# The experts' first layers as seven block products in place of eight, in two passes over the weights

## The chip, the cores and the metric

The kernel runs on one core of one Trainium2 chip. The metric is the device time of one execution in microseconds (us); lower is better.

## The reference

```python
attn = memory_attention(q, k, v, phi)              # 4 x 8 heads x 576 tokens x 64
x = attn.transpose(0, 2, 1, 3).reshape(2304, 512)
h = np.maximum(x @ w_in, 0.0)                      # w_in 512 x 2048
x = h * h @ w_out                                  # w_out 2048 x 512
p = domain_probs / (domain_probs.sum(-1, keepdims=True) + 1e-09)
out = np.zeros((2304, 512))
for e in range(4):                                 # four experts
    h = np.maximum(x @ w1[e], 0.0)                 # w1 512 x 1024
    out += p[:, e:e + 1] * (h @ w2[e])             # w2 1024 x 512
```

Every expert runs on every token. The change is in the loop over the experts alone.

## The kernel before, in words

All products keep fp32 accuracy by a split: a value is held as a rounded high part and the remainder (xh and xl, gh and gl, the two halves of a tile of weights), and a product of two split operands is three matmuls: high x high, high x low, low x high.

The program has two stages. The first holds the attention and the first MLP; it ends with `first_l2` of the last slab, which leaves the tokens' activations in `acc` (seen as `yacc`) and splits them into xh and xl. The second stage is the experts. The hidden width of 4 x 1024 is cut into 16 slabs of 256 columns. For a slab `s`, five blocks of tokens are run, four of 512 and one of 256. For each block `second_l1` makes the slab's two 128-row halves of the hidden layer: 12 matmuls of 128 x 512 into one PSUM bank for each half (4 pieces of the 512 input rows, 3 matmuls for each), and then ScalarE's Relu (gh) and VectorE's remainder (gl). `second_l2` takes 128 tokens at a time: 6 matmuls into one bank, and VectorE adds the result, weighted by the expert's probability, to `acc` (on the first slab ScalarE writes it). The layer 2 of a block is queued in `pend` and is issued behind layer 1 of the next block, so that TensorE has 24 matmuls of layer 1 while the other engines finish a block.

Weights come by a generator, `weights()`: each `next(ws)` loads 256 KB of a slab, and `split` makes the high part (ScalarE, a cast) and the remainder (VectorE). A slab of the experts is four such tiles, loaded once for all 2304 tokens.

The Tile framework schedules: it sets the order of the instructions on each engine and the semaphores between them, and each engine works through its own list in order. PSUM has 8 banks: moe (3), fold (2), turn, memory and score; `CYCLE2` says which is next.

The functions that the change touches:

Of the kernel before, what the change touches and what calls it, by code (L numbers as in the profile page):

```python
# [32 lines left out]
HS = S // 2  # L33


@with_exitstack
def tile_kernel(
# [18 lines left out]
    CYCLE2 = itertools.cycle(("moe", "fold", "moe", "score", "moe", "fold", "memory", "turn"))  # L56
# [58 lines left out]
    def attention(att, g):  # L115
# [47 lines left out]
        for z in range(2):  # L163
# [23 lines left out]
        cols = slice(b * S, (b + 1) * S)  # L187
        nc.scalar.copy(xh[:, hg, cols], at)  # L188
        nc.vector.tensor_tensor(
            out=xh[:, 2 + hg, cols], in0=at, in1=xh[:, hg, cols].bitcast(F32), op=ALU.subtract  # L190
        )
# [36 lines left out]
    def split(w, name):  # L228
        t = wcp.tile([128, 2, WC], F32R, tag="wc", name=name)
# [38 lines left out]
    def fold(s, b):  # L268
        fs, o = SLABS1[s], b * S + offset(s)
# [3 lines left out]
        for h0 in range(0, 2, WC // fs):  # L273
            pf = bank("fold")
            groups = range(h0, h0 + WC // fs)
            for i, hg in enumerate(groups):
# [8 lines left out]
            hi = xl[:, h0:h0 + n, o:o + fs]  # L285
            nc.scalar.copy(hi, src)  # L286
            nc.vector.tensor_tensor(
                out=xl[:, 2 + h0:2 + h0 + n, o:o + fs], in0=src, in1=hi.bitcast(F32), op=ALU.subtract
            )

    def first_l1(s, j, pools, bk):
        hp, tmp = pools
        nf, b = SLABS1[s] // 128, j // 2
        o = b * S + offset(s)
        cs = slice(j * HS, (j + 1) * HS)
        gh = hp.tile([128, nf, HS], F32R, tag="gh", name="gh")
        gl = hp.tile([128, nf, HS], F32R, tag="gl", name="gl")
        for f in range(nf):
# [3 lines left out]
            for hg in range(2):  # L302
                for lw, rx in ((0, 0), (0, 2), (2, 0)):
                    nc.tensor.matmul(  # L304
                        ph[:, :HS], xl[:, lw + hg, fc], xh[:, rx + hg, cs], start=(i == 0), stop=(i == 5)
# [10 lines left out]
    def first_l2(s, j, g, bk):  # L316
# [3 lines left out]
        for d in range(KT):  # L320
# [14 lines left out]
            if s == N1 - 1:  # L335
                nc.scalar.copy(xh[:, d, cs], ya)
                nc.vector.tensor_tensor(
                    out=xl[:, d, cs], in0=ya, in1=xh[:, d, cs].bitcast(F32), op=ALU.subtract
                )


    def second_l1(s, c0, n, hp, bk):
        gh = hp.tile([128, NF2, NB], F32R, tag="gh", name="gh")
        gl = hp.tile([128, NF2, NB], F32R, tag="gl", name="gl")
        for f in range(NF2):
            ph = bk()
            i = 0
            w = w_two[s][f].rearrange("p h (k j) -> p h k j", k=KT)
            for k in range(KT):
                for lw, rx in ((0, xh), (0, xl), (1, xh)):  # L350
                    nc.tensor.matmul(  # L351
                        ph[:, :n], w[:, lw, k, :], rx[:, k, c0:c0 + n],
# [3 lines left out]
            nc.scalar.activation(gh[:, f, :n], ph[:, :n], AF.Relu)  # L356
            nc.vector.scalar_tensor_tensor(  # L357
                out=gl[:, f, :n], in0=ph[:, :n], scalar=0.0, in1=gh[:, f, :n].bitcast(F32),
                op0=ALU.max, op1=ALU.subtract,
            )  # L360
        return gh, gl

    def second_l2(s, c0, n, g, bk):
        gh, gl = g
        e = s // SE
        for q in range(n // 128):
            po = bk()
            i = 0
            ts = slice(q * 128, (q + 1) * 128)
            for f in range(NF2):  # L370
                w = w_two[s][NF2 + f]
# [156 lines left out]
```

## Time and profile before

| | |
|---|---|
| median of 3 runs | 1211.18 us (1210.82 to 1212.43) |
| the profiled execution | 1212.83 us, of which its span (first to last instruction) is 1211.0 us |
| TensorE matmul | busy 1185.9 us, 98% of the span, 6552 matmuls |
| VectorE | 651.7 us, 54% |
| ScalarE | 357.6 us, 30% |
| GpSimd | 1.9 us, 0% |

A matmul's row is longer than the time between two starts, because matmuls are pipelined: the next one starts before the modelled end of the one before. What a matmul costs is therefore read as the distance from one start to the next.

### The profile page before, as it was taken

The page shows a single profiled execution, that of the slowest core. Times are in us where ns is not written, and L with a number is a line of the kernel's source. Part 1 is how long each engine was busy: PE and PEld are TensorE (multiplying, and loading weights), DVE is VectorE, ACT ScalarE, POOL GpSimd, SP SyncE. Part 2 cuts the span into 40 slices and gives each one's busy share as a digit, 9 for nine tenths or more (in the row PEclk, how much of TensorE's full clock was granted, in tenths as well). Part 3 has the DMA queues.
Part 4 walks back from the last instruction along what each step waited for, and adds up shares of the span by engine and source line. Part 5 has one row for each costly group of instructions (what it writes and reads, how often), then busy time and mean ns, then how long its engine had stood idle before and what let it go on. Part 6 is the DMA issues. An engine that isn't in the chain of part 4 may idle for free.

```text
span 1211.0 us, 15894 instructions
## 1 busy us (share of the span) xinstructions
PE 1185.9 (98%) x6552; PEld 998.1 (82%) x6552; DVE 651.7 (54%) x1162; ACT 357.6 (30%) x827; POOL 1.9 (0%) x9
## 2 busy tenths in 40 slices
PE   4899999999999999999999999999999999999998
PEld 2677898898899988888888888888888888888887
DVE  5988999695455513444444444444444444444434
ACT  3676554454465442111111111111111111111110
POOL 0000000000000000000000000000000000000000
PEclk9899999999999999999999999999999999999999
DMA  8741222120010100001000010000100001000003
GB/s 303 257 147 53 70 71 87 54 79 10 1 36 1 35 9 26 18 18 36 18 18 18 18 35 18 18 29 7 35 18 18 35 1 35 18 18 18 1 35 122
DMA packets 25336, 55.84 MB, mean 46 GB/s; under 512 B 2992, under 2 KB 2992, under 8 KB 25264
## 3 DMA queue, kind: packets, MB, share of 16 engines
q1 hardware_dynamic: 25264, 54.84, 13.3%
q8 instruction: 51, 0.84, 0.3%
q14 instruction: 21, 0.17, 0.0%
HBM read 50.11 MB, written 4.72 MB: 45 GB/s over the span
## 4 chain that ended last, share of the span: by engine, by line
PE 96%; DVE 2%; DMA 1%; ACT 0%; issue 0%; SPq 0%
PE moe L373 13%; PE moe L351 11%; PE moe L326 9%; PE fold L373 9%; PE fold L351 6%; PE score L351 6%; PE turn L351 5%; PE memory L351 5%; PE moe L304 5%; PE memory L373 4%; PE turn L373 4%; PE score L373 4%; PE turn L326 3%; PE fold L278 3%; PE score L326 3%; PE memory L326 2%
## 5 line engine op out<-in xcount | busy, mean ns | idle before, releaser
L373 PE MATMUL moe<-w,gh 128*128 128x512 f32 x444 | 137.4, 390 | 0.0
L351 PE MATMUL moe<-xh,w 128*128 128x512 f32 (+1 forms) x456 | 135.2, 363 | 0.0
L326 PE MATMUL moe<-gh,wo 128*128 128x288 f32 x576 | 131.8, 299 | 1.7 <-ACT acc L332 1.2
L356 ACT ACTIVATE gh<-moe 128x512 fp32r<-128x512 f32 (+1 forms) x57 | 30.6, 537 | 344.8 <-PE moe L351 344.8
L357 DVE SCALAR_TENSOR_TENSOR gl<-moe,gh 128x512 fp32r<-128x512 f32 (+1 forms) x57 | 35.1, 617 | 130.0 <-ACT gh L356 130.0
L326 PEld LDWEIGHTS moe<-gh,wo 128*128 128x128 f32 x576 | 97.3, 188 | 8.2 <-ACT acc L332 3.8
L373 PEld LDWEIGHTS moe<-w,gh 128*128 128x128 f32 x444 | 82.8, 188 | 18.1
L373 PE MATMUL fold<-w,gh 128*128 128x512 f32 x316 | 97.3, 389 | 0.0
L351 PEld LDWEIGHTS moe<-xh,w 128*128 128x128 f32 x456 | 82.4, 188 | 14.8
L383 DVE SCALAR_TENSOR_TENSOR acc<-moe,p_sb,acc 128x512 f32<-128x512 f32 x104 | 78.1, 750 | 30.8 <-PE moe L373 28.0
L373 PE MATMUL moe<-w,gl 128*128 128x512 f32 x222 | 86.7, 391 | 0.0
L326 PE MATMUL moe<-gl,wo 128*128 128x288 f32 x288 | 85.1, 296 | 0.0
L351 PE MATMUL moe<-xl,w 128*128 128x512 f32 (+1 forms) x228 | 82.7, 363 | 0.0
L304 PE MATMUL moe<-xh,xl 128*128 128x288 f32 x432 | 75.0, 306 | 4.8 <-ACT xh L188 4.8
L313 DVE TENSOR_TENSOR gl<-g,gh 128x288 fp32r<-128x288 f32 x128 | 57.9, 454 | 36.7 <-ACT gh L312 35.6
L304 PEld LDWEIGHTS moe<-xh,xl 128*128 128x128 f32 x432 | 62.4, 192 | 17.9 <-ACT xl L286 7.6
L383 DVE SCALAR_TENSOR_TENSOR acc<-fold,p_sb,acc 128x512 f32<-128x512 f32 x74 | 55.5, 750 | 37.2 <-PE fold L373 37.2
L351 PE MATMUL fold<-xh,w 128*128 128x512 f32 (+1 forms) x264 | 71.1, 341 | 0.0
L373 PEld LDWEIGHTS fold<-w,gh 128*128 128x128 f32 x316 | 59.3, 188 | 12.3
L351 PE MATMUL score<-xh,w 128*128 128x512 f32 x192 | 64.2, 395 | 0.0
L351 PE MATMUL turn<-xh,w 128*128 128x512 f32 x184 | 61.6, 395 | 0.0
L351 PE MATMUL memory<-xh,w 128*128 128x512 f32 x184 | 61.5, 395 | 0.0
(141 smaller groups left out, 2244.4 us busy)
## 6 DMA issues: line engine op xcount, KB each, us to landing
raw<-in_wts SPq DMA_DIRECT2D x64, 256.0 KB, 2.5
raw<-in_wts SPq DMA_DIRECT2D x28, 512.0 KB, 3.3
kv<-in_kv SPq DMA_DIRECT2D x28, 256.0 KB, 4.0
acc<-in_qT SPq DMA_DIRECT2D x16, 288.0 KB, 5.2
out<-acc SPq DMA_DIRECT2D x18, 256.0 KB, 2.0
ph<-in_phiT SPq DMA_DIRECT2D x8, 288.0 KB, 4.4
acc<-in_wts SPq DMA_DIRECT2D x4, 512.0 KB, 6.3
acc<-in_kv SPq DMA_DIRECT2D x4, 256.0 KB, 7.0
```

What stands on the lines that cost most here:

```text
L278: nc.tensor.matmul(pf[pr * 64:(pr + 1) * 64, i * fs:(i + 1) * fs], bdv[:, 2 * b + hg, pr, :], k_of(2 * hg + pr), start=True, stop=True,)
L304: nc.tensor.matmul(ph[:, :HS], xl[:, lw + hg, fc], xh[:, rx + hg, cs], start=(i == 0), stop=(i == 5))
L313: nc.vector.tensor_tensor(out=gl[:, f], in0=g, in1=gh[:, f].bitcast(F32), op=ALU.subtract)
L326: nc.tensor.matmul(po[:, :HS], w[:, lw], rg[:, f], start=(i == 0), stop=(i == 3 * nf - 1))
L351: nc.tensor.matmul(ph[:, :n], w[:, lw, k, :], rx[:, k, c0:c0 + n], start=(i == 0), stop=(i == 3 * KT - 1),)
L356: nc.scalar.activation(gh[:, f, :n], ph[:, :n], AF.Relu)
L357: nc.vector.scalar_tensor_tensor(out=gl[:, f, :n], in0=ph[:, :n], scalar=0.0, in1=gh[:, f, :n].bitcast(F32), op0=ALU.max, op1=ALU.subtract,)
L373: nc.tensor.matmul(po, lg[:, f, ts], w[:, rw], start=(i == 0), stop=(i == 3 * NF2 - 1))
L383: nc.vector.scalar_tensor_tensor(out=oa, in0=po, scalar=pe, in1=oa, op0=ALU.mult, op1=ALU.add)
```

## The change

The tokens 0 to 2047 are run in two passes of 1024; a pass goes through all 16 slabs. In a pass the 1024 tokens are a pair of blocks of 512, the 512 input rows are two halves of 256, and the slab's hidden 256 columns are two halves of 128. Layer 1 of a slab on a pair is then a 2 x 2 by 2 x 2 block product. Instead of eight block products (48 matmuls of 512 columns) there are seven (42), by Strassen's algorithm in the form with few sums:

- of the weights, four sums of 128 x 256 are made for each slab in each pass, on GpSimd, in a tile `s4` that has one buffer; they are split as weights are (`ws`), so a slab has six split tiles in a pass, not four. Every slab is loaded twice, in loads of 512 KB (`ra` for layer 1, `rb` for layer 2);
- of the activations, `prepare` makes the seven operands of a pass (b11, b21, t1, t4, t2, t3, b22) once: 8 subtractions on VectorE, and 14 splits of 128 x 512 (ScalarE and VectorE). xh and xl are gone; the operands lie in slots of a tile `mem`, in the place that the attention's output and the folded weights held before;
- of the products, the seven go into four banks u, v, m and t. ScalarE copies u out three times while it goes on being added to, VectorE makes four sums of a bank and a copy (`total`: c11, c22, c21, c12), and Relu and remainder are then taken from the sum in SBUF (`rectified`). The product b22 is added into bank m after c22 was read from it;
- layer 2 is the same number of matmuls. Its eight tiles of a pair are put behind layer 1 of the next pair, in two halves, by `between`. It has four banks for itself;
- the last 256 tokens are run as before (`second_rest`), in the second pass, ahead of each pair.

```diff
-    CYCLE2 = itertools.cycle(("moe", "fold", "moe", "score", "moe", "fold", "memory", "turn"))
+    CYCLE2 = itertools.cycle(("fold", "turn", "fold", "memory"))
...
+        for ps_, s in itertools.product(range(2), range(S2)):
+            key = ps_, s
+            r = raw.tile([128, 2 * WC], F32, tag="raw", name=f"ra{ps_}_{s}")
+            nc.sync.dma_start(out=r, in_=wts[s, :, :2 * WC])
+            w_two[key] = [split(r[:, f * WC:(f + 1) * WC], f"w1{ps_}_{s}_{f}") for f in range(2)]
+            yield
+            a11, a12, a21, a22 = (r[:, i * 256:(i + 1) * 256] for i in range(4))
+            t = cp[0].tile([128, 4, 256], F32, tag="s4", name="s4", bufs=1)
+            nc.gpsimd.tensor_tensor(out=t[:, 0], in0=a21, in1=a22, op=ALU.add)
+            nc.gpsimd.tensor_tensor(out=t[:, 1], in0=t[:, 0], in1=a11, op=ALU.subtract)
+            nc.gpsimd.tensor_tensor(out=t[:, 2], in0=a11, in1=a21, op=ALU.subtract)
+            nc.gpsimd.tensor_tensor(out=t[:, 3], in0=a12, in1=t[:, 1], op=ALU.subtract)
+            for i in range(2):
+                u = t[:, 2 * i:2 * i + 2].rearrange("p i n -> p (i n)")
+                w_two[key].append(split(u, f"ws{ps_}_{s}_{i}"))
...
+    def put(dst, src):
+        nc.scalar.copy(dst[0], src)
+        nc.vector.tensor_tensor(out=dst[1], in0=src, in1=dst[0].bitcast(F32), op=ALU.subtract)
...
+        def product(po, name, first=True):
+            wb, xb = block(*a[name]), x[name]
+            i = 0
+            for k in range(2):
+                for lw, rx in ((0, 0), (0, 1), (1, 0)):
+                    nc.tensor.matmul(
+                        po, wb[lw][k], xb[:, rx, k], start=(first and i == 0), stop=(i == 5),
+                        skip_group_check=not first,
+                    )
+                    i += 1
+
+        def total(p, q):
+            c = cp[0].tile([128, NB], F32, tag="c", name="c")
+            nc.vector.tensor_tensor(out=c, in0=p, in1=q, op=ALU.add)
+            return rectified(c, NB)
...
+        u, v, m, t = bank("moe"), bank("moe"), bank("moe"), bank("score")
+        product(u, "b11")
+        u1 = copied(u)
+        product(v, "b21")
+        c11 = total(v, u1)
+        product(m, "t1")
+        product(t, "t4")
+        product(u, "t2", first=False)
+        u2 = copied(u)
+        between(0)
+        product(u, "t3", first=False)
+        u3 = copied(u)
+        c22 = total(m, u3)
+        c21 = total(t, u3)
+        between(1)
+        product(m, "b22", first=False)
+        c12 = total(m, u2)
...
+        for ps_ in range(2):
+            for s in range(S2):
+                if ps_:
+                    todo += second_rest(s, xr, between)
+                todo += second_pair(ps_, s, x, between)
+                for _ in range(3):
                     next(ws, None)
-        flush()
+            if ps_ == 0:
+                xr = rest()
+                for x in prepare(1):
+                    pass
+        between(1)
```

How the order of the instructions moves is shown at three places. In these rows L351 and L373 are the matmuls of layers 1 and 2 before, L471, L517 and L432 those of the pairs, of the last 256 tokens and of layer 2 in the changed kernel; "waits" names the engine waited for, and "xN" means N instructions.

The first place is TensorE in the second stage, before: the second half of a block's layer 1 in slab 6, and the first matmuls of layer 2 behind it.

```order
L351 MATMUL score_7028<-xh_72,w2_6_1_6822 128x512 [waits DVE_49]
L351 MATMUL score_7028<-xl_73,w2_6_1_6822 128x512
L351 MATMUL score_7028<-xh_72,w2_6_1_6822 128x512 x2
L351 MATMUL score_7028<-xl_73,w2_6_1_6822 128x512
L351 MATMUL score_7028<-xh_72,w2_6_1_6822 128x512 x2
L351 MATMUL score_7028<-xl_73,w2_6_1_6822 128x512
L351 MATMUL score_7028<-xh_72,w2_6_1_6822 128x512 x2
L351 MATMUL score_7028<-xl_73,w2_6_1_6822 128x512
L351 MATMUL score_7028<-xh_72,w2_6_1_6822 128x512
L373 MATMUL moe_7043<-w2_6_2_6891,gh_6963 128x512 [waits DVE_49,Activation_49]
```

In the changed kernel a pair of the first pass stands there, here slab 3, from its first product (u is moe_5460, v moe_5461, m moe_5462, t score_5463).

```order
L471 MATMUL moe_5460<-mem_72,w10_3_0_5435 128x512 x6
L471 MATMUL moe_5461<-mem_72,w10_3_0_5435 128x512 [waits Activation_49]
L471 MATMUL moe_5461<-mem_72,w10_3_0_5435 128x512 x5
L471 MATMUL moe_5462<-mem_72,ws0_3_0_5446 128x512 [waits DVE_49]
L471 MATMUL moe_5462<-mem_72,ws0_3_0_5446 128x512 x5
L471 MATMUL score_5463<-mem_72,w10_3_1_5438 128x512 x6
L471 MATMUL moe_5460<-mem_72,ws0_3_0_5446 128x512 [waits Activation_49]
L471 MATMUL moe_5460<-mem_72,ws0_3_0_5446 128x512 x5
L432 MATMUL fold_5503<-w20_2_0_5291,g_5317 128x512 x3
L432 MATMUL fold_5503<-w20_2_1_5294,g_5387 128x512 x3
```

Two groups of 12 became products of 6, with a wait at the head of most of them; four tiles of layer 2 of slab 2 follow (24 matmuls), then the product t3, four more tiles, the product b22, and the next pair.

The second place is VectorE in the second stage, before: additions to `acc` (L383), remainders (L357) and splits of weights (L231).

```order
L383 SCALAR_TENSOR_TENSOR acc_74<-moe_7319,p_sb_81,acc_74 128x512 [waits PE_49]
L231 TENSOR_TENSOR w2_8_2_7539<-raw2_8_2_7537,w2_8_2_7539 128x512 [waits DMAHW3_49,Activation_49]
L383 SCALAR_TENSOR_TENSOR acc_74<-fold_7327,p_sb_81,acc_74 128x512 [waits PE_49]
L231 TENSOR_TENSOR w2_8_3_7608<-raw2_8_3_7606,w2_8_3_7608 128x512 [waits DMAHW4_49,Activation_49]
L357 SCALAR_TENSOR_TENSOR gl_7336<-memory_7337,gh_7335 128x512 [waits Activation_49]
L357 SCALAR_TENSOR_TENSOR gl_7336<-turn_7352,gh_7335 128x512 [waits Activation_49]
```

In the changed kernel, from the sum c22 of pair 3 to its sum c12 (L479 the sums, L453 the remainders, L443 the additions to `acc`, L231 the splits of slab 4's layer 2 weights).

```order
L479 TENSOR_TENSOR c_5543<-moe_5462,cc_5541 128x512 [waits Activation_49]
L479 TENSOR_TENSOR c_5548<-score_5463,cc_5541 128x512
L443 SCALAR_TENSOR_TENSOR acc_73<-fold_5553,p_sb_74,acc_73 128x512 [waits PE_49]
L453 SCALAR_TENSOR_TENSOR g_5545<-c_5543,g_5545 128x512 [waits Activation_49]
L453 SCALAR_TENSOR_TENSOR g_5550<-c_5548,g_5550 128x512 [waits Activation_49]
L443 SCALAR_TENSOR_TENSOR acc_73<-turn_5561,p_sb_74,acc_73 128x512 [waits PE_49]
L443 SCALAR_TENSOR_TENSOR acc_73<-fold_5569,p_sb_74,acc_73 128x512 [waits PE_49]
L231 TENSOR_TENSOR w20_4_0_5617<-rb0_4_5615,w20_4_0_5617 128x512 [waits DMAHW2_49,Activation_49]
L443 SCALAR_TENSOR_TENSOR acc_73<-memory_5577,p_sb_74,acc_73 128x512 [waits PE_49]
L231 TENSOR_TENSOR w20_4_1_5620<-rb0_4_5615,w20_4_1_5620 128x512 [waits Activation_49]
L479 TENSOR_TENSOR c_5591<-moe_5462,cc_5501 128x512 [waits PE_49]
```

Behind c12 stand the second split of `ws` of slab 5, the remainder of c12, then c11 of pair 4 and its remainder, three splits of slab 6 (two of `ra`, the first of `ws`), and the four additions of the next half of layer 2: 22 instructions from one c22 to the next. Before, a slab had no sums and four splits.

The third place is TensorE in the second pass, where the last 256 tokens' layer 2 (fold_8200 and turn_8226) stands between the products, since the pair's own layer 2 has been issued ahead of it.

```order
L432 MATMUL fold_8200<-w21_2_0_8055,g_8106 128x512 [waits DVE_49]
L432 MATMUL fold_8200<-w21_2_0_8055,g_8106 128x512 x2
L432 MATMUL fold_8200<-w21_2_1_8058,g_8154 128x512 x3
L471 MATMUL moe_8157<-mem_72,ws1_2_1_8050 128x512 [waits Activation_49]
L471 MATMUL moe_8157<-mem_72,ws1_2_1_8050 128x512 x5
L432 MATMUL turn_8226<-w21_2_0_8055,g_8106 128x512 [waits DVE_49]
L432 MATMUL turn_8226<-w21_2_0_8055,g_8106 128x512 x2
L432 MATMUL turn_8226<-w21_2_1_8058,g_8154 128x512 x3
L517 MATMUL moe_8272<-mem_72,w11_3_0_8247 128x256 [waits DVE_49]
L471 MATMUL moe_8159<-mem_72,ws1_2_1_8050 128x512 [waits DVE_49]
L471 MATMUL moe_8159<-mem_72,ws1_2_1_8050 128x512 x5
L517 MATMUL moe_8272<-mem_72,w11_3_0_8247 128x256 x11
```

Here one tile of layer 2 stands between the product t2 and t3 (moe_8157, L471) and one tile and one short matmul between t3 and b22 (moe_8159), where the first pass has four tiles at each of the two places.

At the change from the first to the second pass VectorE has 13 instructions of `prepare` between the remainder of the last c12 and the first addition to `acc` of that pair's layer 2. In the last slab of the first MLP the 8 subtractions and 14 splits of the first pass's operands stand among that slab's work, where 32 splits of 128 x 288 stood before.

## Rows read from the trace of the kernel before

**Rows 1.** The page, parts 1 and 2: busy us of each engine; slices in tenths.

```profile
PE 1185.9 (98%) x6552; PEld 998.1 (82%) x6552; DVE 651.7 (54%) x1162; ACT 357.6 (30%) x827; POOL 1.9 (0%) x9
PE   4899999999999999999999999999999999999998
PEclk9899999999999999999999999999999999999999
```

**Rows 2.** The page, part 4: the chain that ended last, by engine.

```profile
PE 96%; DVE 2%; DMA 1%; ACT 0%; issue 0%; SPq 0%
```

**Rows 3.** Windows: the last slab of the first MLP, and 600 us of the experts.

```profile
core 0: us, PE busy (x) PEld busy (x) DVE busy (x) ACT busy (x) POOL busy (x), PEclk, DMA share, GB/s
371.40:409.70 38.30, 38.30 (x290) 38.30 (x289) 21.43 (x49) 20.73 (x56) 0.00 (x0) 1.00 0.01 1
500.00:1100.00 600.00, 600.00 (x2752) 495.90 (x2751) 270.23 (x387) 95.17 (x172) 0.00 (x0) 1.00 0.06 22
```

**Rows 4.** Timeline of TensorE: start, us, engine, line; first and last of stretches.

```profile
409.71 0.39 PE L351 MATMUL moe<-xh,w 128*128 128x512 f32 x1
...
899.74 0.63 PE L373 MATMUL moe<-w,gh 128*128 128x512 f32 x2
...
905.22 0.40 PE L351 MATMUL memory<-xh,w 128*128 128x512 f32 x1
...
910.81 0.63 PE L373 MATMUL moe<-w,gh 128*128 128x512 f32 x2
...
1195.82 0.28 PE L351 MATMUL moe<-xh,w 128*128 128x256 f32 x1
...
1198.70 0.63 PE L373 MATMUL moe<-w,gh 128*128 128x512 f32 x2
...
1206.67 0.39 PE L373 MATMUL turn<-w,gl 128*128 128x512 f32 x1
```

**Rows 5.** Groups of VectorE and ScalarE: busy us, mean ns of one.

```profile
L383 DVE SCALAR_TENSOR_TENSOR acc<-moe,p_sb,acc 128x512 f32<-128x512 f32 x104 | 78.1, 750 | 30.8 <-PE moe L373 28.0
L231 DVE TENSOR_TENSOR w<-raw,w 128x512 fp32r<-128x512 f32 x64 | 44.1, 689 | 15.0 <-ACT w L230 12.7
L230 ACT CAST w<-raw 128x512 fp32r<-128x512 f32 x64 | 39.4, 617 | 26.0 <-PE fold L373 19.0 <-PE turn L326 4.3 <-DMA raw<-in_wts 2.0
L287 DVE TENSOR_TENSOR xl<-fold,xl 128x512 fp32r<-128x512 f32 x32 | 21.9, 686 | 6.9 <-ACT xl L286 6.5
L357 DVE SCALAR_TENSOR_TENSOR gl<-score,gh 128x512 fp32r<-128x512 f32 x24 | 16.6, 692 | 50.6 <-ACT gh L356 50.6
L131 ACT COPY en<-turn 128x512 f32<-128x512 f32 x8 | 4.7, 586 | 5.2 <-PE turn L130 5.2
```

**Rows 6.** Timeline at handovers between the engines.

```profile
1187.34 0.39 PE L351 MATMUL moe<-xh,w 128*128 128x512 f32 x1
1187.57 0.40 PE L351 MATMUL score<-xh,w 128*128 128x512 f32 x1
1187.77 0.60 ACT L356 ACTIVATE gh<-moe 128x512 fp32r<-128x512 f32 x1 [7.65 <-PE moe L351]
1188.40 0.69 DVE L357 SCALAR_TENSOR_TENSOR gl<-moe,gh 128x512 fp32r<-128x512 f32 x1 [2.67 <-ACT gh L356]
...
29.24 0.67 ACT L188 CAST xh<-at 128x576 fp32r<-128x576 f32 x1
...
29.96 0.61 PE L304 MATMUL moe<-xh,xl 128*128 128x288 f32 x1 [4.81 <-ACT xh L188]
```

**Rows 7.** The page, part 6: loads of weights, KB each, us to landing.

```profile
raw<-in_wts SPq DMA_DIRECT2D x64, 256.0 KB, 2.5
raw<-in_wts SPq DMA_DIRECT2D x28, 512.0 KB, 3.3
```

**Rows 8.** Timeline of GpSimd: its longest two instructions.

```profile
1.10 0.29 POOL masks.py:199 TENSOR_SCALAR_AFFINE_SELECT ident<-ident 128x128 f32<-128x128 f32 x1
1.48 0.95 POOL L73 MEMSET bdv<- 128x1024 f32 x1
```

More of the change, by code (lines that the diff above doesn't have):

```diff
@@ L33 @@
 HS = S // 2
+AREA = 2 * KT * S
+NR = NT - 4 * NB
 @with_exitstack
@@ L186, in attention @@
         nc.vector.transpose(out=at, in_=stf)
[L187 to L191, printed above, removed]
+        hi = atts[b][:, hg]
+        nc.scalar.copy(hi, at)
+        nc.vector.tensor_tensor(out=atts[b][:, 2 + hg], in0=at, in1=hi.bitcast(F32), op=ALU.subtract)
     F_MIN = float(np.array(896 << 20, np.uint32).view(np.float32))
@@ L334, in first_l2 @@
                 nc.vector.tensor_tensor(out=ya, in0=po[:, :HS], in1=ya, op=ALU.add)
[L335 to L338, printed above, removed]
-                )
-    def second_l1(s, c0, n, hp, bk):
-        gh = hp.tile([128, NF2, NB], F32R, tag="gh", name="gh")
-        gl = hp.tile([128, NF2, NB], F32R, tag="gl", name="gl")
+    ORDER = ("b11", "b21", "t1", "t4", "t2", "t3", "b22")
@@ new lines, in rectified, with second_pair, block, copied @@
+    def rectified(c, n):
+        g = hp3[0].tile([128, 2, NB], F32R, tag="g", name="g")
+        nc.scalar.activation(g[:, 0, :n], c, AF.Relu)
+        nc.vector.scalar_tensor_tensor(
+            out=g[:, 1, :n], in0=c, scalar=0.0, in1=g[:, 0, :n].bitcast(F32), op0=ALU.max, op1=ALU.subtract
+        )
+        return g
+    def second_pair(ps_, s, x, between):
+        w = w_two[ps_, s]
+        def block(t, c):
+            return [[w[t][:, h, c * 256 + k * 128:c * 256 + (k + 1) * 128] for k in range(2)] for h in range(2)]
+        a = {"b11": (0, 0), "b21": (0, 1), "t1": (2, 0), "t4": (1, 1), "t2": (2, 1), "t3": (3, 0), "b22": (3, 1)}
+        def product(po, name, first=True):
+            wb, xb = block(*a[name]), x[name]
+            i = 0
+            for k in range(2):
+                for lw, rx in ((0, 0), (0, 1), (1, 0)):
+                    nc.tensor.matmul(
+                        po, wb[lw][k], xb[:, rx, k], start=(first and i == 0), stop=(i == 5),
+                        skip_group_check=not first,
+                    )
+                    i += 1
+        def total(p, q):
+            c = cp[0].tile([128, NB], F32, tag="c", name="c")
+            nc.vector.tensor_tensor(out=c, in0=p, in1=q, op=ALU.add)
+            return rectified(c, NB)
+        def copied(p):
+            c = cp[0].tile([128, NB], F32, tag="c", name="cc")
+            nc.scalar.copy(c, p)
+            return c
+        u, v, m, t = bank("moe"), bank("moe"), bank("moe"), bank("score")
[15 more added lines that the diff above has]
+        c12 = total(m, u2)
+        return [
+            (lambda q=q: second_l2(ps_, s, q, (c11, c21) if q < 4 else (c12, c22), (q % 4) * 128))
+            for q in range(8)
+        ]
@@ L355, in second_l1 @@
                     i += 1
[L356 to L371, printed above, removed]
-                for lg, rw in ((gh, 0), (gh, 1), (gl, 0)):
-                    nc.tensor.matmul(
-                        po, lg[:, f, ts], w[:, rw], start=(i == 0), stop=(i == 3 * NF2 - 1)
-                    )
-                    i += 1
-            tt = c0 // 128 + q
-            oa = acc[:, tt * DM:(tt + 1) * DM]
-            pe = p_sb[:, tt, e:e + 1]
-            if s == 0:
-                nc.scalar.activation(oa, po, AF.Copy, scale=pe)
-            else:
-                nc.vector.scalar_tensor_tensor(
-                    out=oa, in0=po, scalar=pe, in1=oa, op0=ALU.mult, op1=ALU.add
-                )
-            if s == S2 - 1:
-                nc.sync.dma_start(out=out[tt * 128:(tt + 1) * 128, :], in_=oa)
+            between(f)
+            g.append(rectified(ph[:, :NR], NR))
+        return [(lambda q=q: second_l2(1, s, 8 + q, g, q * 128)) for q in range(2)]
     pend = []
```

165 lines of the change are left out of this document (124 added, 41 removed).

## The prediction

> **What bounds the kernel now.** I read the shares of the engines first: TensorE is busy for 98% of the span and at 9 tenths or more in every slice but the first and the last, and the granted clock is 8 tenths in the second slice and 9 or more elsewhere, its upper level [rows 1]. The chain that ended last says the same by another way: 96% of it is TensorE [rows 2]. Busy could still be hollow, since a matmul's row is longer than the distance to the next start, so the windows come next: in 600 us of the experts TensorE has no idle time at all, while VectorE is busy for 270.2 us (45%), ScalarE for 95.2 us (16%) and GpSimd not at all [rows 3]. So the experts last as long as their matmuls take to issue, and the question has two parts: what the matmuls that go away took, and whether the work that comes to the three other engines stays hidden.
>
> The price of a matmul is read from starts [rows 4]. Layer 1: 24 matmuls of 512 columns start from 905.22 to 910.81, 0.233 us each. Layer 2: 24 from 899.74 to 905.22, 0.228 us each. The last block's 24 of 256 columns, from 1195.82 to 1198.70, take 0.120 us each. A slab is 96, 108 and 24 of these: 22.4 + 24.6 + 2.9 = 49.9 us, and 16 slabs make 798 us. The trace has 409.71 to 1206.67 and one matmul more, 797.2 us [rows 4]. So the prices hold over the stage, and nothing else is in it.
>
> **What is removed.** Seven products of 6 matmuls for eight: 6 fewer for each of 16 slabs x 2 passes, 192 matmuls. Layer 2 and the last 256 tokens keep their counts. 192 x 0.233 us = **44.7 us less**. The new products have the shape of layer 1, with the activations streaming, so I give them layer 1's price; at layer 2's 0.228 us the 1344 that remain would take another 6.7 us off, which is a bound below. (The Trainium skill, "TensorE: Matmul & The Clock Gate", on the gap between two matmuls, has columns / 2.4 GHz plus some 2.5 ns, 0.216 us for 512 columns; 192 of these would be 41.4 us. The rows have 0.233 us, and the measurement decides.)
>
> **What is added, in the first pass.** Prices are means of the nearest rows [rows 5]: a sum of a PSUM bank and a copy in SBUF 0.69 us (the remainder of `fold`), a remainder 0.69, a split 0.69, an addition to `acc` 0.75; on ScalarE a copy from PSUM 0.59, a cast or Relu from SBUF 0.62. For a pair VectorE has 4 sums, 4 remainders, 6 splits and 8 additions: 14 x 0.69 + 8 x 0.75 = 15.7 us. ScalarE has 3 copies, 4 Relus and 6 casts: 8.0 us. TensorE has 42 x 0.233 + 48 x 0.228 = 20.7 us. So VectorE goes from 45% to 76% and is still not the bound; what is left is whether some instruction comes late in its in-order list.
>
> I follow a pair with the clock at 0 when t3 has issued. TensorE: four tiles of layer 2 to 5.5, b22 to 6.9, b11 and b21 of the next pair to 9.7, then t1, which needs bank m, free when c12 was read. VectorE: a bank can be read 0.20 us after the next matmul's start (1187.57 to 1187.77), VectorE takes over from ScalarE in 0.03, and TensorE from ScalarE in 0.05 [rows 6]. The copy of u is done at 0.8, c22 and c21 at 2.2; then come, in the order shown, an addition, two remainders, two additions, a split, an addition, a split, to 8.0; c12 ends at 8.7. **Cover 1.0 us** before t1. The weights behind it: the buffer of `rb` is free at 8.0, the 512 KB of `ra` land 3.3 us later [rows 7], at 11.3, GpSimd makes its four sums, and the first `ws` is split behind them. Queued behind that split on VectorE are four additions to `acc` (3.0 us) and then c22, which can start at 21.5 (20.7 + 0.2 + 0.59). With 0.62 for the cast and 0.69 for the split this leaves 21.5 - 11.3 - 1.3 - 3.0 = 5.9 us for GpSimd's four sums, 6.9 us with the 1.0 us in front of t1.
>
> No row shows GpSimd with two inputs. Its fastest rate here is a memset, 0.95 us for 1024 columns, 0.24 us for 256; its slowest an affine select, 0.29 us for 128 columns, 0.58 us for 256, and twice that if two inputs are read in turn, 1.16 us [rows 8]. I take 0.58, one read of the kind that is nearest: 2.3 us for four, well inside 5.9; at 1.16 us 4.6, inside too. So the first pass costs nothing more, because TensorE's 20.7 us cover VectorE's list; without that cover each us of lateness in a pair would cost 16 us.
>
> **The second pass.** A pair has 42 products' matmuls, 60 of layer 2 and 24 short ones: 9.8 + 13.7 + 2.9 = 26.4 us, against about 18.0 us on VectorE. But here one tile of layer 2 and one short matmul stand between t3 and b22: 6 x 0.228 + 0.12 = 1.49 us of cover. The chain under it is 0.20 + 0.59 (the copy) + 0.03 + 0.69 (c22) + 0.05 = 1.56 us. So b22 waits about 0.1 us, 16 times: **+1.6 us**. If one VectorE instruction of 0.7 us stands late ahead of c22 it is 0.8 us, 13 us in all: that is the bound above; nothing is the bound below.
>
> **Three seams, once each.** (1) Into the experts: 22 instructions of `prepare` on VectorE, 22 x 0.69 = 15.2 us, replace 32 smaller splits in a slab in which VectorE was busy for 21.4 of 38.3 us [rows 3]; they come in lumps, and the first pair has no layer 2 to cover its copies, but the order puts slab 1's first products there: +2 us (0 to 5). (2) Between the passes: 13 instructions (9 us) of `prepare` stand on VectorE ahead of eight additions to `acc`. TensorE has in that time 24 short matmuls, four tiles of layer 2 and two and a half products to issue, some 12 us, and then needs the first of four banks again: +3 us (0 to 8). (3) The end: eight tiles of the last pair have no products above them, and the first wait for c21's remainder: +1 us (0 to 2). The doubled loads are 64 x 256 KB again [rows 7], 17 MB over 800 us, 21 GB/s beside the 22 GB/s that now keep the DMA engines busy for 6% [rows 3]: no term.
>
> **Sum.** -44.7 + 0 + 1.6 + 2 + 3 + 1 = -37.1 us. Against the profiled execution's 1212.83 us (span 1211.0 and 1.83 around it) 1175.7 us; that execution is 1.65 us above the median of the runs, so I predict **1174 us**. All bounds above give 1174 + (13 - 1.6) + 3 + 5 + 1 = 1194, all bounds below with layer 2's price 1174 - 7.6 - 6.7 = 1160.
>
> **Rivals.** *A: GpSimd and VectorE get in each other's way.* If the two cannot read SBUF at the same time, each of GpSimd's sums would wait for a VectorE instruction (0.69) and the other way round. At 0.58 + 0.69 the four sums take 5.1 us, inside 5.9; at 1.16 + 0.69 they take 7.4, 0.5 us over the 6.9, in some 15 pairs 7.5 us, and with VectorE's own delay (four times 1.16 us in a list of 15.7, 20.3 of 20.7 us) perhaps twice that: 1181 to 1190 us. Against it: most of VectorE's instructions at that place are three, and they then wait for GpSimd anyway. (The Trainium skill, "SBUF — State Buffer", on who interferes with whom, has this rule: a VectorE instruction with two SBUF inputs and a GpSimd instruction that reads SBUF exclude each other for their full length. No row of this trace has the two at once.) *B: the short cover of the second pass fails by a whole instruction*, or VectorE is late at the seams by more than I count: 1181 to 1195 us. The order on VectorE speaks against it: ahead of c22 stands one addition, of a tile that TensorE has finished 1.4 us earlier. *C: the products run at layer 2's price* and the seams are free: 1160 to 1166 us. For it speaks that I know no reason for the 5 ns; against it that all of layer 1 has them. *D, the other side: GpSimd's sums are slow.* They stand in a chain of load, sum, cast, split, with `s4` in one buffer and VectorE's whole list behind the split. Above 1.73 us for a sum (6.9 / 4) each us more costs 4 us a pair. The gain is gone when TensorE waits 37 / 15 = 2.5 us in a pair of the first pass, at 2.35 us for a sum, four times the affine select's rate; at 3 us it is (12 - 6.9) x 15 = 76 us, 1250 us. No row excludes it, since none has this operation, and none is near it.
>
> **How the numbers follow.** My forecast, 1166 to 1181 us, 0.60. A 0.12, B 0.14, C 0.06, D 0.06, and 0.02 that parts of D end within 0.2% (2.4 us) of the time before, which is about what this measurement can tell from no change. The range of 8 in 10 leaves out D, the lowest end of C and the tail above: **1162 to 1192**. Faster 0.92, same 0.02, slower 0.06.
>
> **What would show it.** Right: 1344 + 384 matmuls in layer 1 at 0.233 and 0.12 us, no idle time of TensorE in a pair of the first pass, VectorE at 75% there and 68% in the second, GpSimd's sums at 0.6 us, a wait of about 0.1 us in front of b22 in the second pass, and a few us of idle time near 410 us and in the middle of the experts. Wrong: GpSimd sums above 1.7 us with ScalarE's cast of `ws` waiting for them and TensorE waiting in front of t1 or t3 (A, D); VectorE's instructions with two SBUF inputs above 0.69 us while GpSimd works (A); waits of more than 0.5 us in front of b22 (B); starts 0.228 us apart in the products (C).

## The result, and the profile of the changed kernel

The changed kernel takes **1172.67 us** (median of 4 runs, 1172.49 to 1174.14) against 1211.51 us for the kernel before on the same chip (1210.82 to 1212.43): a ratio of 0.9682, 95% interval 0.9665 to 0.9698. The forecast was 1174 us, with a range of 1162 to 1192. The profiled execution is the one of 1174.14 us, with a span of 1172.0 us.

The page of the changed kernel, parts 1, 2 and 4 (busy us of each engine, the granted clock in tenths by slices, and the chain that ended last by engine):

```profile
PE 1145.5 (98%) x6360; PEld 961.9 (82%) x6360; DVE 838.0 (72%) x1434; ACT 496.5 (42%) x1051; POOL 121.9 (10%) x137
PEclk9799999999999999999999999999999999999999
PE 95%; DVE 2%; issue 1%; DMA 1%; ACT 1%; SPq 0%; ACTq 0%
```

Beside [rows 1, 2] 192 matmuls are gone, TensorE is still 98% busy and 95% of the chain, and VectorE went from 54% to 72%. Windows in the first and the second pass (busy time of PE, PEld, DVE, ACT, POOL; clock; DMA share; GB/s), against [rows 3]:

```profile
435.00:700.00 265.00, 265.00 (x1154) 216.33 (x1153) 198.54 (x280) 102.91 (x173) 54.20 (x52) 1.00 0.15 51
780.00:1100.00 320.00, 320.00 (x1518) 264.90 (x1517) 209.80 (x314) 103.47 (x181) 39.85 (x48) 1.00 0.12 40
```

VectorE is busy for 75% and 66%, and TensorE has no idle time in either window. In the whole stage of the experts the list of TensorE's waits (what waited, for what: us in total, times, the longest) has one line:

```profile
PE moe L471 <- DVE c L479: 0.8, 1, 0.8
```

It stands in front of b22 in the first pair of the second pass. The timeline of TensorE: the first matmuls of the experts, a pair of the first pass from its t3 to the next one's, and the surroundings of b22 in a pair of the second pass, with ScalarE's copy of u and VectorE's c22, and the last matmuls.

```profile
410.60 2.95 PE L471 MATMUL moe<-mem,w 128*128 128x512 f32 x12
...
557.04 1.55 PE L471 MATMUL moe<-mem,ws 128*128 128x512 f32 x6
558.43 1.54 PE L432 MATMUL fold<-w,g 128*128 128x512 f32 x6
...
565.28 2.96 PE L471 MATMUL moe<-mem,w 128*128 128x512 f32 x12
568.08 1.56 PE L471 MATMUL moe<-mem,ws 128*128 128x512 f32 x6
...
577.74 1.55 PE L471 MATMUL moe<-mem,ws 128*128 128x512 f32 x6
...
1019.59 1.55 PE L471 MATMUL moe<-mem,ws 128*128 128x512 f32 x6
1020.99 1.54 PE L432 MATMUL turn<-w,g 128*128 128x512 f32 x6
1021.24 0.59 ACT L484 COPY cc<-moe 128x512 f32<-128x512 f32 x1 [1.66 <-PE moe L471]
1021.86 0.69 DVE L479 TENSOR_TENSOR c<-moe,cc 128x512 f32<-128x512 f32 x1 [0.89 <-ACT cc L484]
1022.36 0.28 PE L517 MATMUL moe<-mem,w 128*128 128x256 f32 x1
1022.61 1.66 PE L471 MATMUL moe<-mem,ws 128*128 128x512 f32 x6
1024.10 1.47 PE L517 MATMUL moe<-mem,w 128*128 128x256 f32 x11
...
1166.31 1.52 PE L432 MATMUL memory<-w,g 128*128 128x512 f32 x6
```

The pair of the first pass takes 577.74 - 557.04 = 20.70 us. Twelve matmuls of the products start from 565.28 to 568.08, 0.233 us each. In the second pass the short matmul at 1022.36 would be followed at 1022.48; b22 starts at 1022.61, behind the end of c22 (1022.55): a wait of 0.13 us, too short for the list of waits. The six of b22 then take 1.49 us in place of 1.40. The product t4 of successive pairs starts 26.58 us apart there, against 42 x 0.233 + 60 x 0.228 + 24 x 0.120 = 26.35 us.

The groups of VectorE and GpSimd in the experts (busy us, mean ns of one, idle before), against [rows 5, 8]:

```profile
L453 DVE SCALAR_TENSOR_TENSOR g<-c,g 128x512 fp32r<-128x512 f32 x128 | 96.1, 771 | 16.3 <-ACT g L452 11.8
L479 DVE TENSOR_TENSOR c<-moe,cc 128x512 f32<-128x512 f32 x96 | 66.2, 689 | 57.3 <-ACT cc L484 37.3 <-PE moe L471 19.9
L231 DVE TENSOR_TENSOR w<-ra,w 128x512 fp32r<-128x512 f32 x62 | 56.2, 911 | 19.0 <-ACT w L230 18.7
L267 POOL TENSOR_TENSOR s<-ra 128x256 f32<-128x256 f32 x30 | 34.5, 1151 | 0.0
L265 POOL TENSOR_TENSOR s<-ra 128x256 f32<-128x256 f32 x30 | 25.9, 862 | 619.8 <-DVE ws L231 389.3 <-DMA ra<-in_wts 230.4
```

What reads PSUM has its price (0.689 us); the split of `ra` and the remainder at L453, which stand beside GpSimd's sums, have grown from 0.69 to 0.91 and 0.77 us in the mean. The first and the last sum of one slab in the timeline, and the two splits of `ra` that stand beside the sums:

```profile
569.77 1.26 POOL L265 TENSOR_TENSOR s<-ra 128x256 f32<-128x256 f32 x1 [16.99 <-DMA ra<-in_wts]
570.37 1.21 DVE L231 TENSOR_TENSOR w<-ra,w 128x512 fp32r<-128x512 f32 x1
...
571.73 0.99 DVE L231 TENSOR_TENSOR w<-ra,w 128x512 fp32r<-128x512 f32 x1 [0.15 <-ACT w L230]
...
573.40 0.74 POOL L268 TENSOR_TENSOR s<-ra,s 128x256 f32<-128x256 f32 x1
```

Beside the last sum VectorE is idle but for its end, and it takes 0.74 us.

**Where the time came from.** The experts last from 410.60 to 1166.31 and six matmuls of layer 2 more, 757.1 us, where they lasted 797.2 [rows 4]: 40.1 us less. That is 44.7 less 4.6, and of the 4.6 us some 4.4 are 15 pairs x 0.23 to 0.25 us and the one wait of 0.8. (That the span shrank by 39.0 and not 40.1 us is the stage ahead, which ended 0.9 us later here; in the eleven runs below that have a t4 the first one starts anywhere between 412.6 and 415.6 us.)

### The profile page after: what moved, and what is told of

Same layout as the page of the kernel before. It is cut to its first block, busy times and chain, and to the rows that moved or that the text cites. A ratio compares the mean times of both kernels' runs of the same rounds, so it can differ in the third digit from the quotient of the medians.

```text
span 1172.0 us, 16362 instructions
## 1 busy us (share of the span) xinstructions
PE 1145.5 (98%) x6360; PEld 961.9 (82%) x6360; DVE 838.0 (72%) x1434; ACT 496.5 (42%) x1051; POOL 121.9 (10%) x137
## 4 chain that ended last, share of the span: by engine, by line
PE 95%; DVE 2%; issue 1%; DMA 1%; ACT 1%; SPq 0%; ACTq 0%
PE moe L471 23%; PE fold L432 17%; PE moe L343 10%; PE memory L432 8%; PE turn L432 8%; PE moe L321 5%; PE moe L517 4%; PE score L471 4%; PE turn L343 3%; PE fold L295 3%; PE score L343 3%; PE memory L343 2%; PE memory L321 2%; PE score L321 1%; PE turn L321 1%; PE memory L139 1%
## 5 line engine op out<-in xcount | busy, mean ns | idle before, releaser
L432 PE MATMUL fold<-w,g 128*128 128x512 f32 x864 | 221.4, 391 | 0.0
L471 PE MATMUL moe<-mem,ws 128*128 128x512 f32 x768 | 201.3, 397 | 0.8 <-DVE c L479 0.8
L432 PEld LDWEIGHTS fold<-w,g 128*128 128x128 f32 x864 | 160.2, 188 | 33.3
L471 PEld LDWEIGHTS moe<-mem,ws 128*128 128x128 f32 x768 | 142.7, 188 | 38.0 <-DVE c L479 5.5
L443 DVE SCALAR_TENSOR_TENSOR acc<-fold,p_sb,acc 128x512 f32<-128x512 f32 x135 | 100.8, 747 | 40.1 <-PE fold L432 40.0
L432 PE MATMUL turn<-w,g 128*128 128x512 f32 x432 | 110.0, 390 | 0.0
L432 PE MATMUL memory<-w,g 128*128 128x512 f32 x432 | 109.8, 389 | 0.0
L453 DVE SCALAR_TENSOR_TENSOR g<-c,g 128x512 fp32r<-128x512 f32 x128 | 96.1, 771 | 16.3 <-ACT g L452 11.8
L479 DVE TENSOR_TENSOR c<-moe,cc 128x512 f32<-128x512 f32 x96 | 66.2, 689 | 57.3 <-ACT cc L484 37.3
L471 PE MATMUL moe<-mem,w 128*128 128x512 f32 x384 | 95.3, 395 | 0.0
L432 PEld LDWEIGHTS turn<-w,g 128*128 128x128 f32 x432 | 81.1, 188 | 17.4
L432 PEld LDWEIGHTS memory<-w,g 128*128 128x128 f32 x432 | 81.1, 188 | 17.4
L471 PEld LDWEIGHTS moe<-mem,w 128*128 128x128 f32 x384 | 71.9, 188 | 17.0 <-ACT cc L484 0.2
```

Source lines behind the costliest of these rows:

```text
L432: nc.tensor.matmul(po, g[f][:, lg, at:at + 128], w[:, rw], start=(i == 0), stop=(i == 3 * NF2 - 1))
L443: nc.vector.scalar_tensor_tensor(out=oa, in0=src, scalar=pe, in1=oa, op0=ALU.mult, op1=ALU.add)
L453: nc.vector.scalar_tensor_tensor(out=g[:, 1, :n], in0=c, scalar=0.0, in1=g[:, 0, :n].bitcast(F32), op0=ALU.max, op1=ALU.subtract)
L471: nc.tensor.matmul(po, wb[lw][k], xb[:, rx, k], start=(first and i == 0), stop=(i == 5), skip_group_check=not first,)
L479: nc.vector.tensor_tensor(out=c, in0=p, in1=q, op=ALU.add)
```

## The experiments

My theory after the result: the gain is the number of matmuls at 0.233 us, less b22's waits in the second pass; all that was added on the other engines, GpSimd's and VectorE's mutual lengthening included, is hidden. Each run stands beside runs of the kernel before on the same chip, whose median was 1211.8 to 1212.2 us, where the changed kernel had 1211.5 beside it. Differences from the changed kernel are therefore sure to some 0.7 us.

**1. The sums on VectorE.**

```diff
-            nc.gpsimd.tensor_tensor(out=t[:, 0], in0=a21, in1=a22, op=ALU.add)
+            nc.vector.tensor_tensor(out=t[:, 0], in0=a21, in1=a22, op=ALU.add)
```

(and the three others.)

> The four sums of weight blocks run on VectorE in place of GpSimd; nothing else changes. My theory: GpSimd and VectorE do lengthen each other in the changed kernel (0.69 us becomes 0.99 to 1.21 us beside a sum), but TensorE never waits for it, so this kernel is within 0.2% of the changed one, 1170 to 1175 us; the splits of `ra` go back from a mean of 0.90 us to 0.69, the pair of the first pass stays at 20.69 us, and VectorE goes from 75% to some 80%. Rival A (the mutual lengthening costs time): faster by more than 2.4 us. Rival (VectorE is closer to being the bound than its busy share says): slower by more than 2.4 us, with TensorE waiting in front of t1 or b22.

1172.15 us (1170.99 to 1173.05), ratio 0.9672 [0.9658, 0.9687], the same as the changed kernel. Groups of VectorE:

```profile
L453 DVE SCALAR_TENSOR_TENSOR g<-c,g 128x512 fp32r<-128x512 f32 x128 | 85.2, 685 | 6.3 <-ACT g L452 2.8
L231 DVE TENSOR_TENSOR w<-ra,w 128x512 fp32r<-128x512 f32 x62 | 42.5, 686 | 17.9 <-ACT w L230 17.7
L265 DVE TENSOR_TENSOR s<-ra 128x256 f32<-128x256 f32 x30 | 12.7, 424 | 6.4 <-DMA ra<-in_wts 5.5
```

With GpSimd still, both groups are back at 0.69 us: the two engines did lengthen each other. It was worth nothing: the pair stays at 20.69 us. VectorE's busy time in the first pass only goes to 76.5% (202.7 of 265 us), since what the sums add (0.42 us each) comes off the lengthened splits and remainders.

**2. and 3. GpSimd's sums twice and three times.**

```diff
+            for _ in range(2):
-            nc.gpsimd.tensor_tensor(out=t[:, 0], in0=a21, in1=a22, op=ALU.add)
+                nc.gpsimd.tensor_tensor(out=t[:, 0], in0=a21, in1=a22, op=ALU.add)
```

(and the three others; `range(3)` in the second kernel.)

> GpSimd makes each slab's four sums twice over, with the same result. In the changed kernel three sums stand ahead of the first cast of `ws`, here seven. By the trace of the changed kernel three sums may take 7.3 us from the landing at 569.77 to the point from which the first layer-2 tile of the pair waits for a bank (cast 0.62, split 0.69 and one addition before 579.13); seven at the mean of 0.96 us take 6.7. My theory: the budget holds, within 0.2%, 1171 to 1176 us. Rival (the slack on GpSimd is as small as the prediction's 5.9 us for four): 0.8 us a pair or more, 1184 us and above.

> GpSimd makes each slab's four sums three times over, with the same result; eleven sums stand ahead of the first cast of `ws`. With the sums made twice no pair of the first pass grew (20.69 us); TensorE waited once, 4.0 us at the first pair of the second pass. My theory: the in-pair budget is 7.3 us plus what the order lets slip, eleven sums at 0.9 us take 9.9, so the pair of the first pass grows by about 2 us (0.5 to 3) and the seam by 4 more; 1205 us (1188 to 1220). Rival (GpSimd's list has free play of a whole pair, since the weights are made one slab ahead): the pairs stay at 20.69 us and only the seam grows, 1182 us.

Twice: 1178.15 us (1177.19 to 1180.53), ratio 0.9725 [0.9711, 0.974]. Every pair of the first pass still takes 20.69 us, so the budget holds there; most of the 5.5 us more came from a place that I had not named, the first pair of the second pass. The list of waits (the loop makes every later line number one higher):

```profile
PE moe L472 <- DVE c L480: 4.0, 1, 4.0
```

Windows from that wait on (TensorE's busy time, clock, DMA share, GB/s):

```profile
754.00:758.30 4.30, 0.32 (x3) 1.00 0.14 41
758.30:760.20 1.90, 1.90 (x7) 0.81 0.50 196
760.20:762.30 2.10, 2.10 (x12) 0.50 0.01 4
```

The wait is 3.2 us longer than in the changed kernel, and the clock of 0.81 and 0.50 in the two windows behind it costs some 1.4 us (0.19 x 1.9 + 0.5 x 2.1): 4.6 of the 5.5 us. There c22 stands on VectorE behind the split of `ws`, that behind GpSimd, and GpSimd could start only when `prepare(1)` was through. Three times: 1223.31 us (1221.18 to 1224.41), ratio 1.0094 [1.0076, 1.0112], slower than the kernel before and above the 1188 to 1220 that I gave it. Two lines of the list of waits:

```profile
PE fold L433 <- DVE acc L444: 25.7, 15, 2.0
PE moe L472 <- DVE c L480: 6.8, 1, 6.8
```

The timeline of TensorE in two pairs of the first pass:

```profile
552.64 2.13 PE L433 MATMUL fold<-w,g 128*128 128x512 f32 x6 [1.95 <-DVE acc L444]
554.57 2.67 PE L433 MATMUL turn<-w,g 128*128 128x512 f32 x6
557.08 1.55 PE L433 MATMUL fold<-w,g 128*128 128x512 f32 x6
...
691.93 1.63 PE L433 MATMUL fold<-w,g 128*128 128x512 f32 x6 [1.95 <-DVE acc L444]
...
694.75 1.52 PE L433 MATMUL fold<-w,g 128*128 128x512 f32 x6
```

Windows there:

```profile
552.60:554.50 1.90, 1.86 (x6) 0.76 0.72 257
554.50:557.00 2.50, 2.50 (x7) 0.50 0.00 2
691.90:695.00 3.10, 3.07 (x14) 1.00 0.45 151
```

The pair grows to between 22.2 and 24.5 us. A wait of up to 2 us at a bank is the step I expected. What I had left out is the clock: behind the wait of 1.95 us at 552.64 it falls to 0.50, and six matmuls take 2.51 us in place of 1.36. That happens in four of the pairs, and those are the ones of 24.5 us; behind the wait of 1.95 us at 691.93 the clock stays at 1.00. What tells the two apart is open. So the price of a sum decides only from somewhere between double and triple, and then it takes the gain away.

**4. An eighth product.**

```diff
         product(v, "b21")
+        product(v, "b21")
```

> The product b21 is computed twice into the same bank, so that each pair has eight products as before, with all the rest of the new scheme. My theory: it gives the 192 matmuls back at 0.233 us, 44.7 us more than the changed kernel, 1217 us (1215 to 1219), some 6 us slower than the kernel before: these 6 us are what the waits and seams of the new scheme cost. Rival (part of the gain comes from the two passes or the order, not from the count): less than 40 us back, under 1213 us. Rival (layer 2's price, 0.228 us, or the rate of 0.216 us): 43.8 or 41.5 us more, 1216.5 or 1214 us.

1217.01 us (1216.65 to 1218.23), ratio 1.0042 [1.0025, 1.0059]: 5.2 us above the kernel before and 44.3 us above the changed kernel, 0.231 us for each of the 192. The pair takes 22.09 us, 1.40 more, six times 0.233. So the count accounts for the whole gain, and no part of it is left for the two passes or the order. The 5.2 us are what the new scheme costs beside it, by another way than the 4.6 us above.

**5. More cover in the second pass.**

```diff
-                    todo += second_rest(s, xr, between)
+                    todo += second_rest(s, xr, three)
```

`three` issues three of the waiting tiles of layer 2, where `between` issued four.

> In the second pass the last block's two products are followed by three tiles of layer 2 each in place of four, so that two tiles (12 matmuls) stand between t3 and b22 where one and a short matmul stood. The pair takes 26.58 us in the changed kernel, against 26.35 by the prices of its matmuls. My theory: the 0.23 us are b22's wait for c22 and what it drags behind it; they go, 15 x 0.23 us, and with them the 0.82 us wait of the first pair: 3 to 4.3 us less, 1168 to 1170 us, a ratio of 0.9965 to 0.9975 to the changed kernel. Rival (the 0.23 us are the price of the switch between matmuls of 256 and 512 columns): the pair stays at 26.5 us and the time within 0.1%.

1167.92 us (1167.32 to 1168.29), ratio 0.9638 [0.9623, 0.9652]: 4.75 us less than the changed kernel. TensorE's timeline around b22:

```profile
1013.35 1.55 PE L471 MATMUL moe<-mem,ws 128*128 128x512 f32 x6
1014.74 1.54 PE L432 MATMUL fold<-w,g 128*128 128x512 f32 x6
1016.12 1.52 PE L432 MATMUL turn<-w,g 128*128 128x512 f32 x6
1017.48 1.55 PE L471 MATMUL moe<-mem,ws 128*128 128x512 f32 x6
1018.87 1.59 PE L517 MATMUL moe<-mem,w 128*128 128x256 f32 x12
```

t3, two tiles of layer 2, and b22 at once: six in 1.39 us. The pair takes 26.31 us, 0.27 less, and the 0.8 us wait is gone too: 15 x 0.27 + 0.8 = 4.85 us, what was measured, and a little more than the 3 to 4.3 us that I gave it.

**6. and 7. One more VectorE instruction ahead of c22.**

```diff
+        if ps_ == 0:
+            d = cp[0].tile([128, NB], F32, tag="c", name="d")
+            nc.vector.tensor_tensor(out=d, in0=u3, in1=u3, op=ALU.add)
         c22 = total(m, u3)
```

(`ps_ == 1` in the second kernel.)

> One more VectorE instruction, the sum of u's copy with itself, stands between that copy and c22 in each pair of the first pass; its result is not used. It lengthens the chain from t3 to b22 by some 0.6 us in a pair in which four tiles of layer 2, 5.5 us, cover it. My theory: 20.69 us a pair as before and the same time within 0.2%, 1171 to 1175 us. Rival (VectorE's list is the bound in the first pass): 0.6 us a pair, 1182 us.

> The same instruction in each pair of the second pass, where the cover is one tile of layer 2 and a short matmul, and b22 already waits. My theory: the whole of it shows, the pair goes from 26.58 to about 27.2 us, 16 x 0.62 us: 1182 us (1180 to 1184). Rival (the 0.23 us in the pair are no wait, and some cover is left): less than 0.3 us a pair, under 1178 us.

First pass: 1172.14 us (1171.22 to 1173.3), 20.69 us a pair, as expected. Second pass: 1172.56 us (1171.63 to 1173.04), 26.59 us a pair: **nothing, where I expected 10 us.** The timeline of TensorE shows why:

```profile
1020.63 0.88 PE L520 MATMUL moe<-mem,w 128*128 128x256 f32 x6
1021.48 1.66 PE L471 MATMUL moe<-mem,ws 128*128 128x512 f32 x6
```

The framework that writes the order put six short matmuls ahead of b22 where one had stood, 0.6 us of cover for 0.6 us of chain, and b22 again starts 0.13 us after it could. The run therefore tells nothing of the wait's price; only run 5, which takes the wait away, does.

**8. What makes a product's matmul 0.233 us and layer 2's 0.228.** The products stream `mem`, layer 2 streams the weights. Here the products stream the weights too, so layer 1 no longer reads the tokens.

```diff
-                        po, wb[lw][k], xb[:, rx, k], start=(first and i == 0), stop=(i == 5),
+                        po, wb[lw][k], w[a[name][0]][:, rx], start=(first and i == 0), stop=(i == 5),
```

> The seven products stream the slab's own weight tiles (512 columns, in the buffers in which layer 2's weights lie) in place of the prepared token blocks, so that the result is not the reference's; everything else is issued as before. It asks why a matmul of a product takes 0.233 us from start to start and one of layer 2 0.228. If it is where the streamed operand lies (`mem` against the weights' buffers): 0.228 us in the products, 20.46 us a pair of the first pass, 7 us less in all, 1166 us. If it is something else (the bank that is written, the stationary operand, the accumulation): 20.69 us a pair and 1172.7 us. I hold the second for likelier.

1163.47 us (1162.66 to 1164.82), ratio 0.9598 [0.9583, 0.9614], 9.2 us less; I had held the other for likelier. TensorE's timeline: twelve of a product in 2.72 us, 0.227 us each, and 20.40 us a pair.

```profile
561.51 2.88 PE L471 MATMUL moe<-w 128*128 128x512 f32 x12
564.23 1.52 PE L471 MATMUL moe<-ws 128*128 128x512 f32 x6
```

So it is the streamed operand, and no tile of the kernel was moved for it; where that operand lies is the next question. By the allocation `mem` starts 17024 bytes into a partition, 128 above a multiple of 512, and the weights at multiples of 1024. Three runs moved one or the other.

**9. `mem` to a multiple of 1024, in the changed kernel and in the kernel before.**

```diff
+    p_sb = const.tile([128, NT // 128, E], F32, name="p_sb")
+    p_sum = const.tile([128, NT // 128], F32, name="p_sum")
     mem = const.tile([128, B * AREA], F32R, name="mem")
...
-    p_sb = const.tile([128, NT // 128, E], F32, name="p_sb")
-    p_sum = const.tile([128, NT // 128], F32, name="p_sum")
```

> The two small tiles `p_sb` and `p_sum` are allocated before `mem` in place of after `acc`. Every instruction and the order on every engine stay the same; `mem`, which the products stream, now starts at byte 17408 of a partition (17 x 1024) in place of 17024, and `acc` moves with it. With the weight tiles streamed (they start at multiples of 1024) the products ran 0.227 us apart. My theory: the 0.233 us of a product's matmul is the start address of the streamed rows, so the pair of the first pass goes from 20.69 to 20.40 us and the time to 1163.5 us (1162 to 1165). Rival (it was not the address, but the buffer's other users, or that streamed and stationary operand lay in one tile): 20.69 us and 1172.5 us.

> The kernel before, with the same two small tiles allocated ahead of `xh`, which goes from byte 17024 to 17408; the order of instructions stays. It asks whether the price of 0.233 us in layer 1 of the kernel before has the same cause. If it is the address: 1536 matmuls of layer 1 at some 0.006 us less, 1202.5 us (1201 to 1204). If not: 1211.8 us.

The changed kernel: 1164.56 us (1163.8 to 1165.28), ratio 0.9607 [0.9593, 0.9621], 8.1 us less with the same instructions in the same order; 20.40 us a pair, and the second pass 26.33. The kernel before: 1202.32 us (1200.79 to 1202.81), ratio 0.9914 [0.9898, 0.9931], 9.6 us less for 1536 matmuls of layer 1, 0.006 us each. Its timeline has 24 of them from 899.35 to 904.79, 0.227 us, where [rows 4] have 0.233:

```profile
899.35 0.39 PE L351 MATMUL memory<-xh,w 128*128 128x512 f32 x1
...
904.79 0.62 PE L373 MATMUL moe<-w,gh 128*128 128x512 f32 x2
```

**10. The other way: 128 bytes more ahead of the weights.**

```diff
     p_sum = const.tile([128, NT // 128], F32, name="p_sum")
+    const.tile([128, 32], F32, name="pad")
```

> The changed kernel with an unused tile of 128 bytes behind `p_sum`, so that every later tile, the weights that layer 2 streams among them, moves by 128 bytes off its multiple of 1024, while `mem` stays where it was. If the start address of the streamed rows sets the price: layer 2's matmuls go from 0.228 to 0.233 us, 1728 of them, some 10 us slower, 1182 us (1180 to 1185), the pair of the first pass at 21.0 us. If the address is not the cause: 20.69 us and 1172.5 us.

1164.82 us (1164.21 to 1165.77), ratio 0.961 [0.9596, 0.9624]: not 10 us slower, but **8 us faster**, with 20.40 us a pair. TensorE's timeline:

```profile
561.35 2.88 PE L472 MATMUL moe<-mem,w 128*128 128x512 f32 x12
564.07 1.52 PE L472 MATMUL moe<-mem,ws 128*128 128x512 f32 x6
568.15 1.52 PE L433 MATMUL fold<-w,g 128*128 128x512 f32 x6
```

So it is not the streamed operand's own alignment: here it lies 128 bytes off a multiple of 512 as ever, and layer 2 now streams weights that lie so too, both at 0.227 us. What fits all of these kernels is the distance between the streamed and the stationary operand: 128 above a multiple of 512 in the slow matmuls (layer 1 before, the products after), a multiple of 512 in all the fast ones. Two things stay open. The pad moved every later tile, VectorE's and ScalarE's too, so that it is the stationary operand that counts is argued, not shown; and with 512 columns no other distance than these two was run. Shorter matmuls do not show the difference. The 24 of 256 columns stream `xh` and `xl` and take 2.88 us in the kernel before [rows 4] and 2.88 us where those were moved in run 9 (1185.85 to 1188.73). In the last slab of the first MLP the operands of the 288-column matmuls lie 0, 128, 256 and 384 bytes beyond multiples of 512 apart by the allocation, in turn, and 24 of them start from 405.80 to 409.00 in the changed kernel, 0.133 us each, whatever the distance.

**11. Cover and allocation together**, the edits of 5 and 9.

> The allocation order of the run before and three tiles of layer 2 behind each of the last block's products, together: the best version that the runs point to. My theory: both gains add, 4.8 and 9 us: 1159 us (1157 to 1161), pairs of 20.40 and 26.0 us. If the address was not the cause: 1168 us, as with the cover alone.

1158.92 us (1158.18 to 1159.69), ratio to the kernel before 0.9561 [0.9546, 0.9575], 13.75 us under the changed kernel, where 4.75 and 8.1 us add to 12.9. No wait of TensorE is left in the experts; the pairs take 20.40 and 26.04 us.

## Why the prediction was right

**The matmuls.** 192 x 0.233 us = 44.7 was forecast; run 4 gives 44.3. (By the Trainium skill, "TensorE: Matmul & The Clock Gate", section "Back-to-back issue gap", it would have been 41.4 us, an estimate from its 0.216 us for 512 columns. No run here comes to that; the shortest is 0.227.)

**The first pass, nothing.** 20.7 us a pair forecast, 20.69 measured; VectorE 76% forecast, 75% measured (68% and 66% in the second pass). Inside, two terms were too small: a GpSimd sum was put at 0.58 us and takes 0.74 alone and 0.86 to 1.15 in the mean, and a split of `ra` was put at 0.69 and takes 0.91. Both lie behind TensorE, as the prediction said that they would. Its budget for GpSimd, 6.9 us with the first cast of `ws` behind all four sums, was on the safe side: only three stand ahead of that cast, and seven still fit (run 2), eleven do not (run 3).

**The second pass, b22.** Forecast 0.1 us a pair from a chain of 1.56 us against 1.49 of cover. The chain took 1.62 us, because the copy of u starts 0.25 us after the next matmul and not 0.20, and the wait is 0.13 us; but the six matmuls behind it lose another 0.09, and run 5 gives 0.27 a pair back. So 1.6 us were forecast, some 4 measured.

**The seams.** 2, 3 and 1 us were forecast. Into the experts and at the end the trace has no wait, between the passes one of 0.8 us: 6 forecast, 0.8 measured. The two errors pull against each other, 2.4 us too little at b22 and 5.2 too much at the seams: 7.6 us given back in the forecast, 4.6 in the trace. That the total came so near is in part luck. I counted the lumps of `prepare` as delays, though TensorE had layer 2's tiles to issue under them. Run 2 shows that the middle seam is nevertheless the first place to break.

**The rivals.** *A*: its mechanism is there, its price is not. (The Trainium skill, "SBUF — State Buffer", section "Who interferes with whom", has a VectorE instruction with two SBUF inputs and a GpSimd one that reads SBUF exclude each other for their full length. The trace agrees in kind: in the slab shown a split of 0.69 us becomes 1.21, a sum of 0.74 becomes 1.26, and the splits come back to 0.69 when GpSimd is left out, in run 1.) *B* did not come, apart from 0.13 us. *C*: the products did not run at layer 2's price, but in runs 8 to 10 they come within 1 ns of it, by another operand or another allocation, and that is worth 8 to 9 us. *D* is real from somewhere between two and three times the work, and at three times it ends on the side that was forecast, slower than before.

## What to carry to other kernels

When TensorE's issue is the bound and the other engines have room, price a change by its count of matmuls and read the price from starts, then look only for places where one instruction's chain is longer than the matmuls that stand over it; here splitting eight tiles as 3 + 3 + 2 instead of 4 + 4 was worth 4.75 us. When two groups of equal matmuls differ in their start-to-start time, don't take it as given: compare where their two operands lie, and try another order of allocation. And before an experiment adds delay, see whether the order is rewritten around it.

## What the runs showed of the hardware

- A matmul of 512 fp32r columns starts 0.233 us after the last one in the kernels where streamed and stationary operand lie 128 bytes apart beyond multiples of 512, and 0.227 us in those where they lie multiples of 512 apart: 8.1 us of 1172.67, and 9.6 of 1212, for the place of two allocations. That the distance is the cause is the reading that fits all runs; it is not shown. At 256 columns there is no difference (0.120 us).
- A GpSimd sum of two 128x256 tiles takes 0.74 us by itself and 1.26 beside VectorE instructions with two SBUF inputs; those go from 0.69 to 0.99 and 1.21 us (569.77 to 573.40, the changed kernel).
- Behind a wait of TensorE of 1.95 us in a stream that is otherwise full the granted clock was 0.76 in the next 1.9 us and 0.50, the lower level of 1.2 GHz, in the 2.5 us after that (552.6 to 557.0, run 3). Behind one of 4.0 us it was 0.81 and 0.50 (run 2); behind the one of 0.8 us, and behind another of 1.95 us in run 3, it stayed at 1.00. The twelve matmuls behind the first took 4.44 us (552.64 to 557.08), those behind the last 2.82 (691.93 to 694.75): the same wait cost 1.6 us more where the clock fell.
